# Products that share TensorE's array get priority behind the first of their group, and the projection's products come four steps later

## The chip, the cores and the metric

The kernel runs on one core of a Trainium2 chip. The metric is the device time of one execution in microseconds (us), lower is better. The profile is of one execution, taken by the hardware profiler; all times in it are counted from the first instruction.

## The reference

Three stages stand behind each other: soft-capped attention, an expert layer with a squared ReLU, and a soft mixture of eight experts.

```python
scores = scale * np.matmul(q, k.transpose(0, 1, 3, 2))     # q, k, v: (4, 12, 448, 64)
scores = cap * np.tanh(scores / cap)
attn = softmax(scores)                                      # denominator + 1e-9
attn_out = np.matmul(attn, v)
x = attn_out.transpose(0, 2, 1, 3).reshape(1792, 768)

h = x @ w_in                                                # w_in: (768, 2048)
g = s * np.maximum(h, 0.0) ** 2 + b
x2 = g @ w_out                                              # w_out: (2048, 768)

logits = x2 @ phi                                           # phi: (768, 32)
d = softmax(logits, axis=0); c = softmax(logits, axis=1)
slot_input = (d.T @ x2).reshape(8, 4, 768)
slot_out[e] = np.maximum(slot_input[e] @ w1[e], 0.0) @ w2[e]
return c @ slot_out.reshape(32, 768)
```

`w_in` and `w_out` arrive as 64-bit floats and are turned into 32-bit ones on the chip.

## The kernel before

A batch is 448 rows of `x`; there are four. The twelve heads of a batch are taken in three groups of four, so `Q` runs from 0 to 11 over groups, and the heads of a group are two pairs (`j` = 0, 1). A group is worked through in 16 steps (`s`).

*Scores.* The scores of a group stand transposed, keys on the partitions, in four chunks `c` of keys: three of 128 (`c` < `KF`), and a last one of 64 that the two heads of a pair share. q and k are split into a high and a low part (`qh`, `ql`, `kh`, `kl`), and a score is the sum of three products, kh·qh + kh·ql + kl·qh. The contraction is 64 long, so a product fills half of TensorE's rows, and the two heads of a pair (`i` = 0, 1) stand in the two halves of the rows. For the first six groups (`WIDE = 6`) `scores` computes one pair of one chunk at a time: six products. From group 6 on, `visit` computes both pairs of a chunk at once: twelve products, into two PSUM tiles with the tags `sc` and `U`; its last chunk is six products of full height. ScalarE takes tanh of them (line 141 or 168), then exp in place (line 206).

*U.* `weighted` multiplies the exponentials with v: for a chunk eight products, two halves `h` of a head's 64 columns times four heads `i`. A product's result is 32 columns wide, and the four heads go to the four quarters of TensorE's columns. It is called for one chunk at a time in the first batch, for chunks (0, 1) and (2, 3) in groups 3 to 5 (sixteen products each), and for all four chunks in groups 6 to 11 (thirty-two). `sums` adds the exponentials up (`Sm`, line 226), and `finish` divides and splits the result into the high and low part of `x`, which also frees the PSUM tile `U`.

*Hidden.* `hidden` computes `x @ w_in` of a batch in 16 chunks of 128 columns, 18 products each (line 527, `hp`), from weights that ScalarE and VectorE split just before (lines 511 and 512). `turn` transposes the squared ReLU (line 550, `tp`; ScalarE copies it away at line 552), and `post` makes the logits (line 564, `L`) four chunks at a time.

*Conversion.* During the first two batches a generator, `convert`, turns the weights into 32-bit floats on ScalarE (line 372) and VectorE (lines 377, 401, 405). w_out comes in eight units `fh` of 256 rows in one buffer `o`. When a unit is ready, `down` multiplies it with phi (line 457, `pp`, six products), `fold` folds that (`pf`), and three times `wturn` transposes a third of it (`tw`), ScalarE copies it back (line 477), and a DMA takes it to a scratch tensor in memory (line 478). The next unit's conversion waits for these DMAs, since there is one buffer `o`. The products are called through the list `self.later`; before it is worked off, the generator yields `HOLD` times. In the first two batches one `next(self.conv)` is made for each third of a chunk of hidden. After the last unit `bias` makes a sum of `pw` (`bp`).

*Order.* `block` weaves `hidden`, `post`, `attention` and `convert` together by calling their generators in turn. What is called earlier has the higher priority; a scheduler then lays out each engine's instructions in order, taking of those that its model holds ready the one of highest priority. On the chip each engine runs its list in that order. `high_priority(n)` moves what is made within it n places ahead, and `issue_after(x)` puts it behind x.

The last 110 us are the experts (`tail`), which stream 54 pieces of weights of 1 MB each (w_out, w1, w2); the first 17 are asked for during the fourth batch, one after another behind its products.

Of the kernel before, what the change touches and what calls it, by code (L numbers as in the profile page):

```python
# [17 lines left out]
P = 128  # L18
B, H, S, D = 4, 12, 448, 64
# [14 lines left out]
KF = S // P  # L34
# [6 lines left out]
LAST = 3  # L41
CASTS = 8
LEAD = 10
WIDE = 6
VISITS = (4, 7, 10, 13)
U = 256
CU = 768
HOLD = 2
XPOS = (1, 4, 7, 10, 13, 15, 15, 15)
POSTS = [[(), (), (0,), (1,)], [(-2,), (-1,), (0, 1), (2,)], [(-1,), (0,), (1,), (2,)], [(-1,), (0,), (1,), (2,)]]  # L50
OUT_GROUPS = [(0, 4), (4, 6)]
# [8 lines left out]
class Body:  # L60
    def __init__(self, nc, tc, io, consts, general, f64, wsc, osc):
        self.nc, self.tc, self.io, self.c, self.general = nc, tc, io, consts, general
        self.f64, self.wsc, self.osc = f64, wsc, osc
        self.ws, self.wr = {}, {}
        self.x = {}
        self.qk = {}
        self.r2 = {}
        self.e = {}
        self.v = {}
        self.nslot = 0  # L70
        self.later, self.wide, self.nsplit = [], False, 0
        self.nx = 0
        self.mark = None
        self.raws = 3

    def bank(self, name):
        return self.pst[0].tile([P, 512], F32, tag="T", bufs=self.pst[1], name=name)
# [48 lines left out]
    def scores(self, p, c):  # L126

        nc = self.nc
        Q, j = divmod(p, 2)
        qh, ql, kh, kl = self.qk[p]  # L130
        sc = (self.ps2 if self.ps2 is not None and j else self.psa).tile([P, 2, 512], F32, tag="sc", bufs=1, name="sc")
        for n, (k, q) in enumerate(((kh, qh), (kh, ql), (kl, qh))):
            if c == KF:
                nc.tensor.matmul(sc[:, 0, :S], k[:, KF * P:], q, start=(n == 0), stop=(n == 2))
            for i in range(2) if c < KF else ():
                r = slice(64 * i, 64 * i + 64)
                nc.tensor.matmul(sc[:, i, :S], k[r, c * P:(c + 1) * P], q[r, :], start=(n == 0), stop=(n == 2))  # L137
        if j == 0:
            self.e.setdefault(Q, []).append(self.ap.tile([P, 4 if c < KF else 2, S], F32, tag="e", bufs=4 if self.general else 3, name="e"))
        if c < KF:  # L140
            nc.scalar.activation(self.e[Q][c][:, 2 * j:2 * j + 2, :], sc[:, :, :S], AF.Tanh, scale=self.c["tsc"])  # L141
        else:
            nc.scalar.activation(self.e[Q][c][:, j, :], sc[:, 0, :S], AF.Tanh, scale=self.c["tsc"])
        if c == NCH - 1:
            del self.qk[p]

    def visit(self, Q, c):

        nc = self.nc
        t = [self.qk[2 * Q + j] for j in range(2)]  # L150
        if c == KF:
            sc = self.psa.tile([P, 2, 512], F32, tag="sc", bufs=1, name="sc")
            for j, (qh, ql, kh, kl) in enumerate(t):
                for n, (k, q) in enumerate(((kh, qh), (kh, ql), (kl, qh))):
                    nc.tensor.matmul(sc[:, j, :S], k[:, KF * P:], q, start=(n == 0), stop=(n == 2))
            self.e[Q].append(self.ap.tile([P, 2, S], F32, tag="er", bufs=1, name="er"))
            nc.scalar.activation(self.e[Q][c], sc[:, :, :S], AF.Tanh, scale=self.c["tsc"])
            del self.qk[2 * Q], self.qk[2 * Q + 1]
            return
        sc = [self.psa.tile([P, 2, 512], F32, tag=n, bufs=1, name="sc") for n in ("sc", "U")]  # L160
        for j, (qh, ql, kh, kl) in enumerate(t):
            for n, (k, q) in enumerate(((kh, qh), (kh, ql), (kl, qh))):
                for i in range(2):
                    r = slice(64 * i, 64 * i + 64)
                    nc.tensor.matmul(sc[j][:, i, :S], k[r, c * P:(c + 1) * P], q[r, :], start=(n == 0), stop=(n == 2))  # L165
        self.e.setdefault(Q, []).append(self.ap.tile([P, 4, S], F32, tag="e", bufs=3, name="e"))
        for j in range(2):
            nc.scalar.activation(self.e[Q][c][:, 2 * j:2 * j + 2, :], sc[j][:, :, :S], AF.Tanh, scale=self.c["tsc"])  # L168
# [65 lines left out]
    def weighted(self, Q, chunks):  # L234

        nc = self.nc
        if chunks[0] == 0:
            self.U = self.psa.tile([P, 2, 512], F32, tag="U", bufs=1, name="U")
        for k in chunks:
            for h in range(2):  # L240
                for i in range(4):
                    d = (i % 2 * KF + k if k < KF else 2 * KF) * D + 32 * h
                    nc.tensor.matmul(self.U[32 * i:32 * i + 32, h, :S], self.v[2 * Q + i // 2][self.rows(i, k), d:d + 32], self.chunk(4 * Q + i, k),  # L243
                                     start=(k == 0), stop=(k == KF))

    def finish(self, Q):

# [17 lines left out]
    def attention(self):  # L265
# [13 lines left out]
        for Q in range(last + 1):  # L279
            for s in range(2 * STEPS):  # L280
# [3 lines left out]
                elif Q < last:  # L284
# [5 lines left out]
                    self.between(Q, s)  # L290
                if not self.general and 0 < Q <= WIDE and s == 1:
                    self.add(Q - 1, 3)
                if not self.general and 0 < Q <= WIDE and s == 3:
                    self.sums(Q - 1)
# [4 lines left out]
    def wide_at(self, Q):  # L299

        return not self.general and Q >= WIDE

# [51 lines left out]
    def convert(self, units):  # L354
# [26 lines left out]
        for n in range(N + 1):  # L381
            if n:
                units[n - 1][2](out.pop(n - 1))
            late = n < N and n not in out
            for _ in range(HOLD if self.later and late else 0):
                yield
# [399 lines left out]
    def block(self, bi, atn):  # L786
# [5 lines left out]
        for grp in range(4):  # L792
# [6 lines left out]
            for k in range(12):  # L799
                next(h)  # L800
                next(post, None)
                if bi < 2:
                    next(self.conv, None)
                while done < min(total, (12 * grp + k + 1) * total / (48 - LEAD)):
                    next(atn)
# [242 lines left out]
```

## Time and profile before

| | |
|---|---|
| median of 3 runs | 642.76 us (639.36, 642.76, 643.01) |
| the profiled execution | 638.93 us, of which the span of its instructions is 637.2 |
| TensorE (PE) busy | 593.7 us, 93% of the span |
| ScalarE (ACT) busy | 402.1 us, 63% |
| VectorE (DVE) busy | 343.4 us, 54% |
| mean granted TensorE clock | 0.988 |

PE is TensorE's products, PEld its weight loads, which run beside the products. Products are pipelined, so a row's length is longer than what it costs: the cost of a piece of work is read from the start of its first row to the start of the next piece. The full-precision products (U, Sm, L, pp) leave two records each, those of scores and hidden one. In the rows' names buffer numbers are left out.

### The profile page before, as it was taken

To read this page: it belongs to the slowest core of one execution; us is meant where nothing else is said; L and a number is where in the kernel's file an instruction comes from. 1 tells how busy PE (TensorE), PEld (TensorE's weight loads), DVE (VectorE), ACT (ScalarE), POOL (GpSimd) and SP (SyncE) were. 2 spreads that over 40 slices of the span, in tenths; PEclk is the share of its full clock that TensorE was granted. 3 is DMA by queue.
4 is the path that set the end of the run, shared out by engine and by line. 5 is a ranking of instruction groups with operands and counts; after the bars stand their busy time and mean duration, and the time that the engine had idled before them with its cause. 6 is when DMAs were issued, how large, how long until landed. Compare 5 with 4: busy or idle time off the path is not lost.

```text
span 637.2 us, 11290 instructions
## 1 busy us (share of the span) xinstructions
PE 593.7 (93%) x4592; PEld 396.3 (62%) x4592; DVE 343.4 (54%) x509; ACT 402.1 (63%) x683; POOL 4.1 (1%) x11
## 2 busy tenths in 40 slices
PE   8898999999999999999999999999999998998672
PEld 5333575746776747567687476768868884346461
DVE  4998899878894482844624825454332224112121
ACT  5887889879867959679569386866645662001010
POOL 1000000000000000000000000000000000000000
PEclk9998999999999999999999999999999999999997
DMA  8843778786685442221421221211968859999998
GB/s 297 290 128 115 269 262 300 252 274 199 235 299 198 136 154 83 87 78 50 141 75 52 84 75 40 72 54 56 394 256 313 315 190 394 421 419 417 419 412 318
DMA packets 39626, 137.38 MB, mean 216 GB/s; under 512 B 4352, under 2 KB 12304, under 8 KB 32656
## 3 DMA queue, kind: packets, MB, share of 16 engines
q1 hardware_dynamic: 39280, 136.07, 59.2%
q8 instruction: 38, 0.62, 0.4%
q0 software_dynamic: 288, 0.53, 0.2%
q14 instruction: 20, 0.16, 0.1%
HBM read 118.49 MB, written 18.09 MB: 214 GB/s over the span
## 4 chain that ended last, share of the span: by engine, by line
PE 65%; DMA 14%; DVE 9%; ACT 8%; issue 3%; SPq 0%; DVEq 0%; ACTq 0%
PE hp L527 32%; DMA wt<-in_w_dram 12%; PE U L243 9%; PE tp L550 4%; PE sc L165 3%; PE pt L640 2%; PE L L564 2%; PE sc L137 2%; PE Sm L226 2%; ACT e L206 2%; ACT e L168 1%; PE tw L475 1%; DVE rec L232 1%; DMA osc<-o 1%; PE pp L457 1%
## 5 line engine op out<-in xcount | busy, mean ns | idle before, releaser
L527 PE MATMUL hp<-x,ws 128*128 128x448 f32 x1152 | 271.4, 376 | 0.0
L527 PEld LDWEIGHTS hp<-x,ws 128*128 128x128 f32 x1152 | 206.4, 188 | 42.2 <-issue 29.4
L512 DVE TENSOR_TENSOR ws<-wr,ws 128x384 fp32r<-128x384 f32 x128 | 70.6, 553 | 123.3 <-ACT ws L511 123.1
L511 ACT CAST ws<-wr 128x384 fp32r<-128x384 f32 x128 | 66.8, 524 | 36.8 <-PE hp L527 36.3
L243 PE MATMUL U<-e,v 128*32 128x448 f32 (+1 forms) x672 | 75.8, 551 | 4.7 <-ACT e L206 3.7
L206 ACT ACTIVATE e<-e,c_acap 128x1792 f32<-128x1792 f32 (+1 forms) x42 | 71.5, 1702 | 0.5
L552 ACT COPY g<-tp 112x256 f32<-112x256 f32 x128 | 43.3, 385 | 12.8 <-PE tp L550 12.0
L243 PEld LDWEIGHTS U<-e,v 128*32 128x32 f32 (+1 forms) x672 | 20.7, 110 | 45.4 <-issue 36.3
L232 DVE RECIPROCAL rec<-rec 128x448 f32<-128x448 f32 x12 | 35.4, 2950 | 18.1 <-ACT rec L231 18.1
L141 ACT ACTIVATE e<-sc,c_tsc 128x896 f32<-128x896 f32 x36 | 35.9, 1008 | 12.9 <-PE sc L137 11.9
L533 ACT ACTIVATE r<-hp 128x448 f32<-128x448 f32 x63 | 34.9, 554 | 9.8 <-PE hp L527 9.8
L550 PE MATMUL tp<-c_cst,r 128*112 128x128 f32 x256 | 39.0, 275 | 1.7 <-ACT g L552 1.4
L897 ACT COPY wt<-op 128x512 f32<-128x512 f32 x12 | 7.0, 586 | 50.6 <-PE op L892 50.6
L168 ACT ACTIVATE e<-sc,c_tsc 128x896 f32<-128x896 f32 x36 | 36.1, 1035 | 4.0 <-PE sc L165 4.0
L534 ACT ACTIVATE r<-r 128x448 f32<-128x448 f32 x63 | 37.6, 596 | 0.4
L912 PE MATMUL so_ps<-wt,free 128*32 128x128 f32 x768 | 26.5, 282 | 10.9 <-DMA wt<-in_w_dram 10.5
L550 PEld LDWEIGHTS tp<-c_cst,r 128*112 128x112 f32 x256 | 29.5, 133 | 11.3 <-ACT g L552 3.8
L215 DVE TENSOR_TENSOR es<-e 128x1792 f32<-128x1792 f32 x12 | 24.3, 2022 | 13.7 <-ACT e L206 13.7
L912 PEld LDWEIGHTS so_ps<-wt,free 128*32 128x32 f32 x768 | 20.8, 113 | 15.2 <-DMA wt<-in_w_dram 12.8
L215 DVE TENSOR_TENSOR es<-es,e 128x1792 f32<-128x1792 f32 x12 | 24.3, 2022 | 9.6 <-ACT e L206 9.6
L231 ACT ACTIVATE rec<-Sm,c_eps 128x448 f32<-128x448 f32 x12 | 7.7, 638 | 28.9 <-PE Sm L226 28.9
L863 PE MATMUL hps<-wt,free 128*32 128x512 f32 x192 | 21.0, 593 | 0.0
(186 smaller groups left out, 705.9 us busy)
## 6 DMA issues: line engine op xcount, KB each, us to landing
wt<-in_w_dram SPq DMA_DIRECT2D x48, 1024.0 KB, 16.5
wr<-wsc SPq DMA_DIRECT2D x48, 384.0 KB, 3.1
raw<-in_w_in_dram SPq DMA_DIRECT2D x16, 768.0 KB, 5.2
raw<-in_w_outT_dram SPq DMA_DIRECT2D x16, 768.0 KB, 5.8
wsc<-wr SPq DMA_DIRECT2D x16, 384.0 KB, 3.0
osc<-o SPq DMA_DIRECT2D x24, 256.0 KB, 2.9
wt<-osc SPq DMA_DIRECT2D x6, 1024.0 KB, 7.0
k<-in_kT_dram SPq DMA_DIRECT2D x22, 256.0 KB, 3.4
```

Source lines behind the costliest of these rows:

```text
L168: nc.scalar.activation(self.e[Q][c][:, 2 * j:2 * j + 2, :], sc[j][:, :, :S], AF.Tanh, scale=self.c["tsc"])
L206: ins = self.nc.scalar.activation(e, e, AF.Exp, scale=self.c["acap"]).ins
L215: self.nc.vector.tensor_add(es, e[0] if c == 1 else es, e[c])
L232: nc.vector.reciprocal(self.rec, self.rec)
L243: nc.tensor.matmul(self.U[32 * i:32 * i + 32, h, :S], self.v[2 * Q + i // 2][self.rows(i, k), d:d + 32], self.chunk(4 * Q + i, k), start=( ...
L511: self.nc.scalar.copy(hi, u)
L512: self.nc.vector.tensor_sub(lo, u, hi.bitcast(F32))
L527: nc.tensor.matmul(hp[:, :S], ws[kc // 3][:, w, kc % 3, :], x[:, s, kc, :], start=(k == 0), stop=(k == 3 * KC - 1))
L534: self.mark = nc.scalar.activation(r2, r2, AF.Square).ins
L550: self.nc.tensor.transpose(tp[:CP, q * P:(q + 1) * P], r2[:, q * CP:(q + 1) * CP], self.c["idn"])
L552: self.nc.scalar.copy(self.g[q][:CP, :, fc * P:(fc + 1) * P], tp[:CP, 2 * q * P:2 * (q + 1) * P].rearrange("p (a b) -> p a b", b=P))
L912: nc.tensor.matmul(so_ps[32 * e:32 * e + 32, G, :], ht[G][:, f, 32 * e:32 * e + 32], w2[f // 4][:, f % 4, e, :], start=(f == 0), stop=(f = ...
```

## The change

A helper `together` takes a list of products. It issues the first as before, and all others with a priority 3000 places ahead, and behind the first. The scores of pairs from the third on (`scores` with p ≥ 2, and `visit`) and U from group 3 on go through it. `visit` also takes the terms in another order, kl·qh first and kh·qh last, and in its last chunk the second pair first. `HOLD` becomes 4, so `down`, `fold` and `wturn` of a unit are called two steps of the generator later than before.

```diff
+VISIT = 3000
-HOLD = 2
+HOLD = 4
...
+    def together(self, products, near=True):
+
+        if not near:
+            products = [f() for f in products]
+            return
+        first, rest = products[0](), products[1:]
+        with self.tc.issue_after(first.ins), self.tc.high_priority(VISIT):
+            for p in rest:
+                p()
...
     def scores(self, p, c):
...
-        for n, (k, q) in enumerate(((kh, qh), (kh, ql), (kl, qh))):
-            if c == KF:
-                nc.tensor.matmul(sc[:, 0, :S], k[:, KF * P:], q, start=(n == 0), stop=(n == 2))
-            for i in range(2) if c < KF else ():
-                r = slice(64 * i, 64 * i + 64)
-                nc.tensor.matmul(sc[:, i, :S], k[r, c * P:(c + 1) * P], q[r, :], start=(n == 0), stop=(n == 2))
+        products = [lambda n=n, k=k, q=q, i=i, r=r: nc.tensor.matmul(sc[:, i, :S], k[r, c * P:(c + 1) * P], q[r, :], start=(n == 0), stop=(n == 2))
+                    for n, (k, q) in enumerate(terms) for i, r in halves]
+        if p < 2:
+            for f in products:
+                f()
+        else:
+            self.together(products)
...
     def visit(self, Q, c):
...
-            for j, (qh, ql, kh, kl) in enumerate(t):
-                for n, (k, q) in enumerate(((kh, qh), (kh, ql), (kl, qh))):
-                    nc.tensor.matmul(sc[:, j, :S], k[:, KF * P:], q, start=(n == 0), stop=(n == 2))
+            self.together([lambda j=j, n=n, k=k, q=q: nc.tensor.matmul(sc[:, j, :S], k[:, KF * P:], q, start=(n == 0), stop=(n == 2))
+                           for j, (qh, ql, kh, kl) in reversed(list(enumerate(t))) for n, (k, q) in enumerate(((kl, qh), (kh, ql), (kh, qh)))])
...
-        for j, (qh, ql, kh, kl) in enumerate(t):
-            for n, (k, q) in enumerate(((kh, qh), (kh, ql), (kl, qh))):
-                for i in range(2):
-                    r = slice(64 * i, 64 * i + 64)
-                    nc.tensor.matmul(sc[j][:, i, :S], k[r, c * P:(c + 1) * P], q[r, :], start=(n == 0), stop=(n == 2))
+        half = [slice(64 * i, 64 * i + 64) for i in range(2)]
+        self.together([lambda j=j, n=n, k=k, q=q, i=i, r=r: nc.tensor.matmul(sc[j][:, i, :S], k[r, c * P:(c + 1) * P], q[r, :], start=(n == 0), stop=(n == 2))
+                       for j, (qh, ql, kh, kl) in enumerate(t) for n, (k, q) in enumerate(((kl, qh), (kh, ql), (kh, qh))) for i, r in enumerate(half)])
...
     def weighted(self, Q, chunks):
...
+        self.together(products, Q >= 3)
```

Three places of TensorE's order show it; a row is a line of the program, the tile written and the tiles read, and how many such instructions follow each other.

TensorE at the second half of U of group 3, before; L is the first batch's logits, pp and tw belong to the unit of w_out that is being converted:

```order
L137 MATMUL sc<-qh,kh 128x448 x2
L243 MATMUL U<-e,v 32x448 x5
L137 MATMUL sc<-ql,kh 128x448 x2
L457 MATMUL pp<-o,c_misc 32x256 x6
L137 MATMUL sc<-qh,kl 128x448 x2
L243 MATMUL U<-e,v 32x448 x4
L475 MATMUL tw<-c_cst,o 128x128 x4
L243 MATMUL U<-e,v 32x448 x7
L527 MATMUL hp<-x_398,ws 128x448 x6
```

and now (the line numbers are those of the changed file):

```order
L237 MATMUL Sm<-es,c_ones 32x448
L256 MATMUL U<-e,v 32x448 x16
L237 MATMUL Sm<-es,c_ones 32x448 x3
L542 MATMUL hp<-x_398,ws 128x448 x6
L565 MATMUL tp<-c_cst,r_817 112x128 x4
L145 MATMUL sc<-qh,kh 128x448 x2
L145 MATMUL sc<-ql,kh 128x448 x2
L145 MATMUL sc<-qh,kl 128x448 x2
L472 MATMUL pp<-o,c_misc 32x256 x6
```

The sixteen products of U stand in one piece instead of three, and the six of the scores too.

TensorE in group 8, where a visit is cut by a transpose, before:

```order
L165 MATMUL sc<-qh,kh 128x448 x2
L165 MATMUL sc<-ql,kh 128x448 x2
L165 MATMUL sc<-qh,kl 128x448 x2
L165 MATMUL sc<-qh,kh 128x448 x2
L550 MATMUL tp<-c_cst,r_2269 112x128 x4
L165 MATMUL sc<-ql,kh 128x448 x2
L165 MATMUL sc<-qh,kl 128x448 x2
```

and now, in the same group:

```order
L175 MATMUL sc<-qh,kl 128x448 x2
L175 MATMUL sc<-ql,kh 128x448 x2
L175 MATMUL sc<-qh,kh 128x448 x2
L565 MATMUL tp<-c_cst,r_2162 112x128 x4
L542 MATMUL hp<-x_1095,ws 128x448 x10
L565 MATMUL tp<-c_cst,r_2246 112x128 x4
L542 MATMUL hp<-x_1095,ws 128x448
L175 MATMUL sc<-qh,kl 128x448 x2
L175 MATMUL sc<-ql,kh 128x448 x2
L175 MATMUL sc<-qh,kh 128x448 x2
```

The pieces are now of whole pairs of heads; the second pair of this visit stands behind ten products of hidden and a transpose.

TensorE between the last `tw` of the seventh unit of w_out and `pp` of the eighth, before:

```order
L475 MATMUL tw<-c_cst,o 128x128 x4
L155 MATMUL sc<-ql,kh 128x448
L155 MATMUL sc<-qh,kl 128x448
L527 MATMUL hp<-x_1095,ws 128x448 x2
L550 MATMUL tp<-c_cst,r_1747 112x128 x4
L527 MATMUL hp<-x_1095,ws 128x448 x4
L243 MATMUL U<-e,v 32x448 x24
L243 MATMUL U<-er,v 32x448 x8
L527 MATMUL hp<-x_1095,ws 128x448 x8
L457 MATMUL pp<-o,c_misc 32x256 x6
```

and now, where `tw`, ten products of hidden and six of scores stand just ahead of these rows:

```order
L542 MATMUL hp<-x_1095,ws 128x448 x19
L175 MATMUL sc<-qh,kl 128x448 x3
L175 MATMUL sc<-ql,kh 128x448 x2
L175 MATMUL sc<-qh,kh 128x448 x2
L175 MATMUL sc<-qh,kl 128x448
L175 MATMUL sc<-ql,kh 128x448 x2
L175 MATMUL sc<-qh,kh 128x448 x2
L542 MATMUL hp<-x_1095,ws 128x448
L175 MATMUL sc<-qh,kl 128x448 x2
L175 MATMUL sc<-ql,kh 128x448 x2
L175 MATMUL sc<-qh,kh 128x448 x2
L472 MATMUL pp<-o,c_misc 32x256 x6
```

U no longer stands between the two; scores and hidden do.

## Rows read from the trace of the kernel before

**Rows 1.** Busy time of each engine by stage: stretch, length, engines, granted clock, DMA

```profile
0.00:66.50 66.50, 57.80 (x419) 26.66 (x419) 54.00 (x78) 52.61 (x56) 2.98 (x9) 0.97 0.60 205
66.50:200.00 133.50, 131.94 (x850) 87.45 (x848) 112.89 (x142) 109.85 (x180) 0.00 (x0) 1.00 0.77 265
200.00:430.00 230.00, 226.46 (x1528) 152.22 (x1525) 121.84 (x166) 170.31 (x293) 0.54 (x1) 1.00 0.28 85
...
528.00:637.20 109.20, 79.66 (x1248) 50.05 (x1246) 23.89 (x64) 11.94 (x22) 0.54 (x1) 0.94 0.99 401
```

**Rows 2.** Who waited for whom, TensorE: us in total, times, longest

```profile
PE U L243 <- ACT e L206: 3.7, 3, 1.6
...
PE pp L457 <- DVE o L405: 2.8, 4, 1.4
...
PE tp L550 <- ACT g L552: 1.4, 3, 0.7
```

**Rows 3.** Groups by line, hidden: busy, mean ns, idle before

```profile
L527 PE MATMUL hp<-x,ws 128*128 128x448 f32 x1152 | 271.4, 376 | 0.0
```

**Rows 4.** Timeline of TensorE, start and length in us: U in one piece

```profile
116.52 3.21 PE L243 MATMUL U<-e,v 128*32 128x448 f32 x32
119.67 0.55 PE L475 MATMUL tw<-c_cst,o 128*128 128x128 f32 x3
```

**Rows 5.** Timeline of TensorE: U in three pieces

```profile
132.85 1.69 PE L243 MATMUL U<-e,v 128*32 128x448 f32 x10
134.47 0.47 PE L137 MATMUL sc<-ql,kh 64*128 64x448 f32 x2
...
136.26 1.82 PE L243 MATMUL U<-e,v 128*32 128x448 f32 x8
138.01 0.66 PE L475 MATMUL tw<-c_cst,o 128*128 128x128 f32 x4
138.60 1.70 PE L243 MATMUL U<-e,v 64*32 64x448 f32 x14
140.23 1.48 PE L527 MATMUL hp<-x,ws 128*128 128x448 f32 x6
```

**Rows 6.** Timeline of TensorE: a visit in two pieces, a transpose between

```profile
284.06 0.47 PE L165 MATMUL sc<-qh,kh 64*128 64x448 f32 x2
...
285.71 0.65 PE L550 MATMUL tp<-c_cst,r 128*112 128x128 f32 x4 [0.58 <-ACT g L552]
286.29 0.48 PE L165 MATMUL sc<-ql,kh 64*128 64x448 f32 x2
...
286.90 0.47 PE L527 MATMUL hp<-x,ws 128*128 128x448 f32 x1
```

**Rows 7.** Timeline of TensorE: a visit in one piece

```profile
292.74 0.47 PE L165 MATMUL sc<-qh,kh 64*128 64x448 f32 x2
...
294.15 0.47 PE L527 MATMUL hp<-x,ws 128*128 128x448 f32 x1
```

**Rows 8.** Timeline of TensorE: a transpose between products of hidden

```profile
295.48 0.60 PE L550 MATMUL tp<-c_cst,r 128*112 128x128 f32 x4
295.83 1.46 PE L527 MATMUL hp<-x,ws 128*128 128x448 f32 x6
```

**Rows 9.** Timeline of all engines: from the seventh unit's last tw to pp

```profile
219.24 0.60 PE L475 MATMUL tw<-c_cst,o 128*128 128x128 f32 x4
...
224.46 1.82 ACT L372 ACTIVATE o<-raw 128x768 f32<-128x768 f32 x2 [0.27 <-DMA osc<-o]
...
230.50 1.06 PE L457 MATMUL pp<-o,c_misc 128*32 128x256 f32 x12 [0.42 <-DVE o L405]
```

**Rows 10.** Waits of SP's DMA queue

```profile
SPq L725 <- DVE ws L512: 11.8, 1, 11.8
```

**Rows 11.** Chain that ended last, its pieces in the tail: start, length in us

```profile
547.52 13.68 DMA wt<-in_w_dram
```

**Rows 12.** Timeline of TensorE: U of group 2, behind a wait

```profile
51.33 3.77 PE L243 MATMUL U<-e,v 128*32 128x448 f32 x16 [0.93 <-DVE c_hh L255]
```

More of the change, by code (lines that the diff above doesn't have):

```diff
@@ L131, in scores @@
         sc = (self.ps2 if self.ps2 is not None and j else self.psa).tile([P, 2, 512], F32, tag="sc", bufs=1, name="sc")
-        for n, (k, q) in enumerate(((kh, qh), (kh, ql), (kl, qh))):
-            if c == KF:
-                nc.tensor.matmul(sc[:, 0, :S], k[:, KF * P:], q, start=(n == 0), stop=(n == 2))
-            for i in range(2) if c < KF else ():
-                r = slice(64 * i, 64 * i + 64)
-                nc.tensor.matmul(sc[:, i, :S], k[r, c * P:(c + 1) * P], q[r, :], start=(n == 0), stop=(n == 2))
+        halves = [(0, slice(0, P))] if c == KF else [(i, slice(64 * i, 64 * i + 64)) for i in range(2)]
+        terms = ((kh, qh), (kh, ql), (kl, qh))
+        products = [lambda n=n, k=k, q=q, i=i, r=r: nc.tensor.matmul(sc[:, i, :S], k[r, c * P:(c + 1) * P], q[r, :], start=(n == 0), stop=(n == 2))
[5 more added lines that the diff above has]
+            self.together(products)
         if j == 0:
@@ L238, in weighted @@
             self.U = self.psa.tile([P, 2, 512], F32, tag="U", bufs=1, name="U")
-        for k in chunks:
+        order = tuple(chunks)
+        products = []
+        for k in order:
             for h in range(2):
@@ L242, in weighted @@
                     d = (i % 2 * KF + k if k < KF else 2 * KF) * D + 32 * h
-                    nc.tensor.matmul(self.U[32 * i:32 * i + 32, h, :S], self.v[2 * Q + i // 2][self.rows(i, k), d:d + 32], self.chunk(4 * Q + i, k),
-                                     start=(k == 0), stop=(k == KF))
+                    products.append(lambda k=k, h=h, i=i, d=d: nc.tensor.matmul(
+                        self.U[32 * i:32 * i + 32, h, :S], self.v[2 * Q + i // 2][self.rows(i, k), d:d + 32], self.chunk(4 * Q + i, k),
+                        start=(k == 0), stop=(k == KF)))
+        self.together(products, Q >= 3)
     def finish(self, Q):
```

## Prediction

> **What bounds the kernel now.** I read the stages first [rows 1]. In the stretch from 66.5 to 200 us TensorE is busy for 131.9 of 133.5 us, from 200 to 430 us for 226.5 of 230: together it idles 5.1 us in 363.5. VectorE is busy for 85% of the first of these stretches and ScalarE for 82%, in the second for 53% and 74%. So TensorE's own list is the time there, and the other two have some room, least before 200 us. The groups by line confirm it: hidden's products never wait, 0.0 us before 1152 of them [rows 3]. The waits that TensorE does have are few: 2.8 us at pp for VectorE's last step on a unit of w_out, 1.4 us at transposes for ScalarE's copy, and 3.7 us at U for exp, these before 25 us [rows 2].
>
> Busy is not the same as used. Sixteen products of U in one piece take 116.52 to 119.67, 3.15 us or 0.79 for four [rows 4]: the four heads run side by side in the quarters of the columns. Where a piece is cut in the middle of a four, the rest of the four is alone and the row still counts as busy. The same holds for scores, whose two heads run side by side. That is what this change can win, and it is read from starts of pieces, not from busy time.
>
> In the last stage the weights of the experts set the time: the DMA engines are 99% busy at 401 GB/s, and the chain there goes through these loads [rows 1, 11]. They begin when buffers of the fourth batch come free: SP's queue of them stands 11.8 us for VectorE's last splits of hidden's weights [rows 10]. So the stage starts when hidden ends, and I let all that is won before it arrive at the end.
>
> **U in one piece.** Before, the second half of U of group 3 stands in three pieces: 132.85 to 134.47, 136.26 to 138.01 and 138.60 to 140.23, together 5.00 us [rows 5], against 3.15 whole [rows 4]: 1.85 us lost. Three more of the twelve U from group 3 on are cut, at 153.70, 175.22 and 351.13; read in the same way they lose 0.85, 0.29 and 0.86. The order now has all twelve whole. Sum: **−3.85 us**, all on TensorE's path.
>
> **Scores in one piece.** A whole visit takes 292.74 to 294.15, 1.41 us for six pairs of products [rows 7]; a piece of two pairs takes 286.29 to 286.90, 0.61 [rows 6]. Solved for both, a pair costs 0.20 and every new piece 0.21. Counted in the two orders from the first product of hidden on, scores stand in 65 pieces before and in 50 now: 15 × 0.21 = 3.1. Six pairs of heads are cut apart before and one now; a cut pair runs as two products of 0.20: 5 × 0.20 = 1.0. Sum **−4.1 us**. The order of the terms, low part first, adds no instruction. It makes the first product wait for the part that is ready last, so that those behind it need no wait of their own; no row before shows a visit of group 6 or later waiting for an operand, so I give it nothing, between 0 and −0.5.
>
> **What moves next to them.** A transpose ahead of hidden costs 0.35 us (295.48 to 295.83 [rows 8]), ahead of scores 0.58 (285.71 to 286.29 [rows 6]). Such neighbours fall from 15 to 8: −1.6 at most; I take −1.2, since some of these 15 cost less than the one shown. Hidden itself stands in 154 pieces instead of 151, 3 × 0.2 = +0.6 at the price of a piece of scores, an estimate. Sum **−0.6 us**.
>
> **Phi's products later.** Two more steps of the generator are two thirds of a chunk of hidden, so `pp` of the second and third unit now has scores or some eight products of hidden more ahead of it. Both waited for VectorE. Of the four waits, 2.8 us in total and the longest 1.4 [rows 2], I expect three to go: −2.4. The fourth, the last unit's, gets worse. From the seventh unit's last tw to that pp it takes 11.26 us [rows 9]: tw, ScalarE's copy, the DMA, whose end releases ScalarE at 224.46, and then 6.04 us of ScalarE and VectorE until pp starts. The tw of the seventh unit is itself later now, and what lies between is 30 products of hidden and 24 of scores in three pieces: 0.35 + 30 × 0.20 + 12 × 0.20 + 3 × 0.21 = 9.4 us. So pp would wait for 11.3 − 9.4 = 1.9 us, instead of 0.4. Sum −2.4 + 1.5 = **−0.9 us**; with the chain at its shortest and all other waits gone −2.8, with a busier VectorE there (U's division and split now stand among its steps) +1. On SP's queue a unit's three stores come later with their tw and change places with loads of q, k, v and of weights by a few rows; hidden, whose weights go through that queue, does not wait now [rows 3], and I give it nothing. `pf`, `bp` and the logits behind it come later too, by up to two chunks of hidden. ScalarE writes a chunk's squared ReLU into one of nine buffers, which the transposes behind the logits free; in the new order the relu of the chunk ten places on stands right behind that transpose. It holds no product of hidden back as long as the other of two PSUM tiles is free, and thirty-two products of U (two of rows 4's pieces, 6.3 us) stand there as cover. I take 0; without that cover it is one wait for ScalarE, 0.7 us if it is as long as the longest at a transpose [rows 2].
>
> **Waits at transposes.** The transpose in [rows 6] waited 0.58 us for ScalarE behind a cut visit, one of three such waits, 1.4 us in total [rows 2]. Transposes still follow visits at several places, so I take half: **−0.7 us**, between 0 and −1.4.
>
> **The first 66 us.** Here VectorE (54.0) and ScalarE (52.6 of 66.5 us) count as much as TensorE. Two single pieces of scores between U's of group 1 and 2 go, 0.4 us each, half of it on the path: **−0.4 us**. The granted clock has a mean of 0.97 here [rows 1], and U of group 2, directly behind a wait of 0.93 us, takes 3.77 us for eight products, where rows 4 have 1.6: it runs at the lower level, 1.2 GHz [rows 12]. Two products of scores now stand ahead of that U and shorten the wait; whether the clock then stays at 2.4 GHz no row says. I take 0, between 0 and −2.2 (3.77 − 1.6).
>
> **New waits.** TensorE's list is shorter by ten us and ScalarE's and VectorE's are not. One place is plain in the order: a visit's second half in group 8 needs the PSUM tile U back, whose sums `Sm` now come some 15 us behind U. The nearest rows are the 5.1 us that TensorE idles in both stretches [rows 1]. I take **+1.5 us**, between 0 and another 5.
>
> **Sum.** −3.85 − 4.1 − 0.6 − 0.9 − 0.7 − 0.4 + 1.5 = −9.05, say −9.1 us. The profiled execution took 638.93 (637.2 of span and 1.7 around it), which gives 629.8. It is at the low end of the runs shown; taken from their median, 642.76, the forecast is **633.7 us**. With the bounds above (−15 to −4) its own range is 628 to 639.
>
> **Rivals.**
>
> *The win turns into waits.* Of the sum, about 5.5 us lie before 200 us (3.0 of U, 1.5 of scores, 1.0 of pp). There VectorE is 85% and ScalarE 82% busy and each of them has its own long operations; if TensorE, 4% earlier, only waits for them, that part is lost and −3.5 us stay: 639. For it: pp's waits are for VectorE. Against it: hidden never waits [rows 3], and shortening 133.5 us by 5.5 puts VectorE at 88%, not at 100. The Trainium skill (TensorEngine Tiling (Array Packing), Performance Considerations, PSUM Bottleneck) says that packing small products speeds up TensorE but not the evacuation of PSUM, which may then become the limit; that speaks for this rival. By that rule the trace of before shows only the start, the 1.4 us at transposes for ScalarE's copy.
>
> *The end does not follow.* If the last stage's loads were paced by memory from the fourth batch on, 99% busy as the DMA engines are, TensorE's gain would end in a longer wait for weights: −1 to 0, 642. Against it: the wait of 11.8 us of their queue for hidden [rows 10].
>
> *Slower: U waits for exp.* Priority draws the products of U for the last chunk right up to the exponentials. TensorE takes its list in order, so each of the twelve U from group 3 on can stand for ScalarE with hidden's products behind it. If ScalarE is late by more than the 4.7 us that the first 24 products of a U take (three quarters of two of rows 4's pieces), each such U waits, as long as the longest wait of U for exp before, 1.6 us in the first stage [rows 2]: 12 × 1.6 = 19 less the 10.6 won, **+9**, 652. Against it: ScalarE at 74% from 200 us on, and before too U starts close behind the last scores.
>
> **Chances.** The forecast 0.62, more than it 0.05, the win turned into waits 0.20, an end that does not follow 0.06, slower through U 0.07. About 1% (6.4 us) is what a measurement of this kernel can tell from no change. Faster by over 1%: the forecast and the case above it, less 0.05 for the part of the forecast's own range that wins under 6.4 us, 0.62; within 1%: that part, the waits and the end that does not follow, 0.31; slower: 0.07. For the range, forecast and waits together hold 0.82: 625 to 642.
>
> **What would show it.** In the changed kernel's trace U from group 3 on should stand in pieces of 3.15 and 6.3 us and visits in 1.4; hidden should still wait 0.0; pp's waits should be one, of 1 to 3 us, near 230 us; the first load behind hidden should start some 9 us earlier. I would be wrong if TensorE's idle time from 66.5 to 430 us grew by more than 5 us, or if the stage of the experts grew longer than 109 us.

## The result and the profile after

| | before | after |
|---|---|---|
| median, this comparison (6 runs each) | 641.84 us (639.36 to 643.01) | 634.48 us (632.77 to 637.68) |
| profiled execution, its span | 638.93, 637.2 | 632.77, 630.9 |
| ratio, 95% interval | | 0.9896 (0.9864 to 0.9928) |
| first product of hidden starts at | 66.49 | 64.26 |
| `ln_ps`, the first products behind the last logits, start at | 528.53 | 522.10 |
| between the two | 462.0 | 457.8 |

The kernel is faster by 1.0%. The same kernel in a second comparison gave 635.14 against 640.62 (below, 0.9931), so the gain is 5.5 to 7.4 us. One execution of hold2, an experiment below, took 1965.88 us; it stands in that kernel's median and not in its ratio.

The first view is the busy time by stage, to be laid beside [rows 1]; the columns are the same.

```profile
0.00:66.50 66.50, 58.71 (x432) 27.98 (x434) 56.37 (x79) 53.91 (x58) 2.99 (x9) 0.95 0.64 217
66.50:200.00 133.50, 131.64 (x870) 89.19 (x867) 111.30 (x143) 114.19 (x185) 0.00 (x0) 1.00 0.76 263
200.00:430.00 230.00, 225.80 (x1532) 151.54 (x1531) 126.38 (x169) 168.42 (x294) 0.54 (x1) 1.00 0.28 84
```

From 66.5 to 430 us TensorE idles 1.9 + 4.2 = 6.1 us, where it was 5.1. ScalarE, the fourth busy time of a row, does more in the second stage than before (114.2 against 109.9), since more of the work now lies there; VectorE a little less. The waits of TensorE, as in [rows 2] (us in total, times, longest):

```profile
PE tp L565 <- ACT g L567: 2.9, 4, 0.9
...
PE U L256 <- ACT e L217: 1.3, 2, 0.9
PE sc L175 <- ACT e L179: 1.1, 2, 0.9
...
PE pp L472 <- ACT g L567: 0.4, 1, 0.4
...
PE pp L472 <- DVE o L420: 0.3, 1, 0.3
```

The product with phi has lost its 2.8 us of waiting for VectorE, and transposes have gained: 2.9 instead of 1.4, all for ScalarE's copy. Visits, of which no wait is listed before, wait 1.1 us for a tanh. U waits for exp at 12.8 and 22.2 us alone. The pieces themselves are as forecast, all but one U (at 129.87 us, shown with sums_too). TensorE's timeline, start and length, shows a U of two chunks from 168.91 to 172.19, 3.28 us, and a U of four from 414.36 to 420.64, 6.28 us ([rows 4]: 3.15 for two), and a whole visit from 406.25 to 407.68, 1.43 ([rows 7]: 1.41):

```profile
168.91 3.35 PE L256 MATMUL U<-e,v 128*32 128x448 f32 x32
172.19 0.66 PE L490 MATMUL tw<-c_cst,o 128*128 128x128 f32 x4
```

```profile
406.25 0.47 PE L175 MATMUL sc<-qh,kl 64*128 64x448 f32 x2
...
407.68 1.49 PE L542 MATMUL hp<-x,ws 128*128 128x448 f32 x6
...
414.36 4.72 PE L256 MATMUL U<-e,v 128*32 128x448 f32 x48
419.01 1.71 PE L256 MATMUL U<-er,v 64*32 64x448 f32 x16
420.64 0.96 PE L237 MATMUL Sm<-es,c_ones 128*32 128x448 f32 x8
```

For the sum by kind I take, for each product of TensorE, the time from its start to the next start, from the first product of hidden to `ln_ps`. Waits are then with the product ahead of them.

| us | before | after | difference |
|---|---|---|---|
| U | 60.65 | 57.63 | −3.0 |
| scores | 57.04 | 52.35 | −4.7 |
| transposes of hidden | 26.25 | 25.30 | −0.95 |
| hidden | 256.63 | 260.67 | +4.0 |
| all else | 61.5 | 61.9 | +0.4 |
| sum | 462.0 | 457.8 | −4.2 |

So U and scores give 7.7 us, and hidden takes back 4.0. Hidden's products take 0.202 us each when nothing holds them; what they take beyond that, by what comes behind the piece, goes from 0.5 to 4.0 us ahead of transposes, from 2.9 to 5.2 ahead of scores, and from 3.9 to 0.7 ahead of the product with phi.

Some of this only changes its place. Before, the transposes that waited stood behind scores, and their waits count there; now they stand behind hidden. So I also take the waits out: for each, the time from the start ahead of it to the start behind it, less what the same two kinds take where nothing waits. Then scores go from 54.5 to 50.85 us (−3.65), hidden from 253.0 to 253.85 (+0.85), and the waits from 6.5 to 8.7 (+2.2); those at transposes from 2.3 to 3.85. The idle time of the profile goes from 5.2 to 6.2 in the same stretch and shows less of it: a row of hidden is 0.376 us long [rows 3] while the next product can start after 0.202, so some 0.17 us of a wait behind it lie under the row.

Three of the new places, in the timelines of all engines. At 333 us:

```profile
331.32 1.94 ACT L179 ACTIVATE e<-sc,c_tsc 128x896 f32<-128x896 f32 x2
...
333.10 0.69 ACT L567 COPY g<-tp 112x256 f32<-112x256 f32 x2
...
333.85 0.65 PE L565 MATMUL tp<-c_cst,r 128*112 128x128 f32 x4 [0.86 <-ACT g L567]
```

The visit comes whole now, and here its two tanh stand directly ahead of the copies that free the tile for the next transpose: 1.94 us of ScalarE. Between the first product of hidden and `ln_ps` that is so at four places, and at none before. But it holds for two of the four waits alone (201.4 and 333.9, 1.57 of the 2.9 us). At 290.2 the copies stand behind three short steps for hidden (288.20 to 289.50), and at 153.2 behind a step of the conversion that itself waited for a store:

```profile
151.72 0.90 ACT L387 ACTIVATE o<-raw 128x768 f32<-128x768 f32 x1 [1.65 <-DMA osc<-o]
152.52 0.62 ACT L567 COPY g<-tp 112x256 f32<-112x256 f32 x2
...
153.19 0.54 PE L565 MATMUL tp<-c_cst,r 128*112 128x128 f32 x3 [0.65 <-ACT g L567]
```

Before, at the longest of these waits, the copies stood behind an exp, nearly as long as two tanh, and a split of weights:

```profile
339.38 1.79 ACT L206 ACTIVATE e<-e,c_acap 128x1792 f32<-128x1792 f32 x1
...
341.48 0.64 ACT L552 COPY g<-tp 112x256 f32<-112x256 f32 x2
...
342.17 0.54 PE L550 MATMUL tp<-c_cst,r 128*112 128x128 f32 x3 [0.71 <-ACT g L552]
```

The third place is at 234 us, where the last unit of w_out is converted:

```profile
229.99 1.69 ACT L387 ACTIVATE o<-raw 128x768 f32<-128x768 f32 x2 [1.62 <-DMA osc<-o]
231.59 0.89 ACT L91 CAST x<-U 128x896 fp32r<-128x896 f32 x1
232.38 0.51 ACT L526 CAST ws<-wr 128x384 fp32r<-128x384 f32 x1
232.79 1.00 ACT L179 ACTIVATE e<-sc,c_tsc 128x896 f32<-128x896 f32 x1
...
233.85 0.67 PE L175 MATMUL sc<-qh,kl 64*128 64x448 f32 x3 [0.87 <-ACT e L179]
```

ScalarE is busy without a gap, and the tanh that frees the scores' PSUM tile is the fourth in its row. The end follows in full. The first load of the chain in the tail (start, length) begins 6.4 us earlier than in [rows 11], and from there to the span's end it is 89.8 us, 89.7 before:

```profile
541.10 13.68 DMA wt<-in_w_dram
```

### The profile page after: what moved, and what is told of

Read it like the earlier page. It is cut to its first block, busy times and chain, and to the rows that moved or that the text cites. A ratio compares the mean times of both kernels' runs of the same rounds, so it can differ in the third digit from the quotient of the medians.

```text
span 630.9 us, 11279 instructions
## 1 busy us (share of the span) xinstructions
PE 587.1 (93%) x4592; PEld 393.5 (62%) x4592; DVE 343.5 (54%) x509; ACT 401.5 (64%) x683; POOL 4.1 (1%) x11
## 4 chain that ended last, share of the span: by engine, by line
PE 58%; DMA 15%; ACT 15%; DVE 8%; issue 3%; SPq 0%; ACTq 0%; DVEq 0%
PE hp L542 29%; DMA wt<-in_w_dram 12%; PE U L256 8%; PE tp L565 4%; ACT e L217 4%; PE sc L175 2%; PE pt L655 2%; ACT e L155 2%; PE L L579 2%; DMA osc<-o 2%; PE Sm L237 2%; ACT e L179 1%; ACT ws L526 1%; PE sc L145 1%; PE tw L490 1%
## 5 line engine op out<-in xcount | busy, mean ns | idle before, releaser
L527 DVE TENSOR_TENSOR ws<-wr,ws 128x384 fp32r<-128x384 f32 x128 | 70.3, 552 | 109.9 <-ACT ws L526 107.3
L526 ACT CAST ws<-wr 128x384 fp32r<-128x384 f32 x128 | 66.6, 524 | 32.7 <-PE hp L542 32.2
L256 PE MATMUL U<-e,v 128*32 128x448 f32 (+1 forms) x672 | 71.0, 551 | 2.1 <-ACT e L217 1.3
L145 PE MATMUL sc<-qh,kh 64*128 64x448 f32 (+1 forms) x84 | 22.2, 464 | 3.6 <-ACT e L155 1.7
L145 PEld LDWEIGHTS sc<-qh,kh 64*128 64x128 f32 (+1 forms) x84 | 9.4, 192 | 19.5 <-issue 6.3
```

The source lines that it names most:

```text
L145: products = [lambda n=n, k=k, q=q, i=i, r=r: nc.tensor.matmul(sc[:, i, :S], k[r, c * P:(c + 1) * P], q[r, :], start=(n == 0), stop=(n == ...
L256: products.append(lambda k=k, h=h, i=i, d=d: nc.tensor.matmul(self.U[32 * i:32 * i + 32, h, :S], self.v[2 * Q + i // 2][self.rows(i, k), d ...
L526: self.nc.scalar.copy(hi, u)
L527: self.nc.vector.tensor_sub(lo, u, hi.bitcast(F32))
```

## The experiments

Those of one group were timed on one chip beside the kernel before, g_both_first on another; the first row has the medians of before beside the change, the three groups and g_both_first. "Stretch" is the time from the first product of hidden to `ln_ps` in the profiled execution, "first" where it begins, "tp" the waits at transposes for the copy `g`, "pp" those at the product with phi.

| kernel | median us | ratio (95%) | first | stretch | tp | pp |
|---|---|---|---|---|---|---|
| before | 641.84, 640.53, 640.62, 640.94, 640.45 | | 66.5 | 462.0 | 1.4 | 2.8 |
| the change | 634.48 | 0.9896 (0.9864 to 0.9928) | 64.3 | 457.8 | 2.9 | 0.7 |
| hold2 | 634.44 | 0.9893 (0.9861 to 0.9926) | 63.8 | 457.9 | 1.9 | 3.8 |
| hold4_only | 642.37 | 1.0027 (1.0008 to 1.0046) | 65.5 | 465.4 | 2.2 | 1.3 |
| u_only | 640.65 | 0.9998 (0.9976 to 1.0019) | 66.6 | 460.3 | 1.7 | 3.6 |
| scores_only | 635.76 | 0.9924 (0.9894 to 0.9953) | 63.9 | 459.5 | 2.2 | 2.8 |
| changed_again | 635.14 | 0.9931 (0.9908 to 0.9954) | 65.0 | 458.0 | 2.8 | 0.9 |
| early_as_before | 634.86 | 0.9924 (0.9903 to 0.9945) | 65.2 | 458.4 | 2.8 | 0.7 |
| high_first | 633.46 | 0.9895 (0.9879 to 0.9912) | 63.8 | 458.6 | 2.7 | 0.3 |
| g_on_dve | 633.87 | 0.9919 (0.9887 to 0.9950) | 63.9 | 458.7 | 3.3 | 0.5 |
| g_both_dve | 632.11 | 0.9873 (0.9847 to 0.9899) | 65.9 | 456.1 | 1.2 | 2.2 |
| g_first | 633.00 | 0.9879 (0.9852 to 0.9907) | 63.9 | 457.1 | 2.7 | 1.4 |
| sums_too | 634.95 | 0.9913 (0.9882 to 0.9943) | 65.9 | 458.5 | 3.3 | 0.9 |
| g_both_first | 631.20 | 0.9857 (0.9836 to 0.9879) | 64.0 | 457.4 | 1.5 | 2.1 |

The first group takes the change apart: grouping of U, grouping of scores, and the four steps.

**hold2**, the change with the old `HOLD`.

```diff
-HOLD = 4
+HOLD = 2
```

> The changed kernel with HOLD back at 2: products stay together, phi's products come as early as before. My account: the gain is mostly the pieces of scores and U and the clock in the first stage; only pp's waits come back, 2 to 3 us, so the ratio to the kernel before is about 0.994 (-4 us) and the wait at pp for VectorE is 2 to 3 us again. Rival, the gain is HOLD's: ratio 0.998 to 1.0.

It is as fast as the change, where the account had 4 us for it and the ratio 0.994. The product with phi waits again, and the transposes wait less by 1 us; the stretch is the same to 0.1 us. The change's waits at 153.2 and 201.4 us, 1.36 us together, are not there; one of 0.71 at 242.6 is new.

```profile
PE pp L472 <- DVE o L420: 2.8, 4, 1.5
PE tp L565 <- ACT g L567: 1.9, 3, 0.9
...
PE pp L472 <- ACT r L549: 1.0, 1, 1.0
```

**hold4_only**, the kernel before with `HOLD = 4` and nothing else.

```diff
-HOLD = 2
+HOLD = 4
```

> The kernel before with HOLD 4 alone. Its order has U from group 3 on in 23 pieces instead of 17 and scores in 62 instead of 65. My account: pp's waits go (-3 us), the six new pieces of U cost 2 to 4 us, so the ratio is 0.997 to 1.002. Rival, the gain is HOLD's: ratio 0.992 or less.

Slower by 0.3%, just outside the account's range, and by 3.3 us in the stretch, though the product with phi waits 1.5 us less: U is cut into more pieces, and its sum by kind is 2.9 us longer, that of `tw` 1.2; that of scores is the same.

**u_only**, U grouped from group 3 on, scores and `HOLD` as before; the edit is shown against the change, and `visit` is put back likewise.

```diff
-        self.together(products)
+        for n, (k, q) in enumerate(((kh, qh), (kh, ql), (kl, qh))):
...
-HOLD = 4
+HOLD = 2
```

> The kernel before with U from group 3 on together, nothing else. My account: -3 to -4 us for the five pieces fewer, ratio 0.995; pp's waits and the clock in the first stage as before. Rival, U's products then wait for exp: U's waits over 2 us more than before and a ratio of 1.0 or more.

U takes 3.7 us less, as forecast for it (3.85), and scores 1.3 more, 1.0 of which are waits behind them; the product with phi waits 0.8 more. The stretch is shorter by 1.7. Of that the medians show nothing (between −1.5 and +1.2 us). The account's ratio is missed; the rival's 1.0 came, but without its cause, since U waits for exp less than before (2.9 us instead of 3.7).

**scores_only**, scores grouped, U and `HOLD` as before.

```diff
-        self.together(products, Q >= 3)
+        self.together(products, False)
...
-HOLD = 4
+HOLD = 2
```

> The kernel before with scores together (and low part first), U and HOLD as before. My account: 16 pieces fewer, -4 us, the clock in the first stage -2 us, waits at transposes +1.5, so ratio 0.993. Rival, what grouped scores win they give back in waits for ScalarE: ratio 0.998 to 1.0, with 3 us or more of waits at transposes and scores.

Scores take 5.6 us less, hidden 3.9 more; with the waits taken out scores take 3.9 less and hidden the same, and the waits grow by 2.9. The stretch falls by 2.5, and the first product of hidden comes 2.6 earlier. This part alone gives most of the change's time. In the stretch the parts add up where `HOLD` is left alone: −1.7 − 2.5 = −4.2, and hold2, which has both, −4.1.

The second group asks what the first stage and the order of the terms are worth, and tries to take ScalarE out of the waits at transposes.

**changed_again**, the change once more, as a measure for the others. 

> The changed kernel once more, as the yardstick of this chip: ratio 0.99, -6 to -7 us; waits at transposes near 3 us and none over 0.5 us at pp, if these are of the program and not of one execution.

Medians of one kernel differ by 0.7 us between the two comparisons, and those of the kernel before by up to 1.4; less than that is not told from noise below.

**early_as_before**, the scores of pairs up to the sixth left as they were.

```diff
-        if p < 2:
+        if p < 6:
```

> The changed kernel with the scores of the first three groups issued as before: TensorE's order up to the first product of hidden is that of the kernel before, behind it that of the changed one. My account: the clock falls again at U of group 2, hidden starts 2 us later, ratio 0.9925. Rival, the clock's fall is chance or hidden in a stage bound by ScalarE and VectorE: ratio 0.9895 to 0.9905, first product of hidden at 64 to 65 us.

The time is that of the change once more, and so is the stretch. The ratio is the one that the account gave, but the fall of the clock that it gave as the reason did not come. Of interest is the clock from 48 to 58 us, where the kernel before ran U of group 2 at the lower level [rows 12]. The windows of 48 to 58 us, of before and of this kernel (the third number from the end is the granted clock):

```profile
48.00:58.00 10.00, 8.56 (x53) 3.10 (x50) 7.05 (x6) 6.76 (x6) 0.00 (x0) 0.83 0.37 126
```

```profile
48.00:58.00 10.00, 8.58 (x66) 3.35 (x66) 8.39 (x9) 8.13 (x9) 0.00 (x0) 1.00 0.36 126
```

With the early scores ungrouped the clock stays up here; it does so in hold4_only too. So what rows 12 show does not come with that order of TensorE every time.

**high_first**, the terms of `visit` in the old order.

```diff
-for n, (k, q) in enumerate(((kl, qh), (kh, ql), (kh, qh)))
+for n, (k, q) in enumerate(((kh, qh), (kh, ql), (kl, qh)))
```

> The changed kernel with visit's terms in the old order, kh first. My account: the order of the terms is worth nothing, ratio within 0.001 of the changed kernel's. Rival, the low part first spares waits within a visit: 1 to 2 us slower, with waits of scores for VectorE's kl in groups 6 to 11.

No loss; its median is below changed_again's by 1.7 us, its stretch the longer one by 0.6. The account's 0.001 is missed beside changed_again (0.9931) and met beside the first comparison (0.9896). The low part first wins nothing that shows; whether the old order is a little faster is not settled, since the two intervals touch.

**g_on_dve**, the second of the two copies behind a transpose on VectorE, from the ninth chunk on and not in the last batch.

```diff
-            self.nc.scalar.copy(self.g[q][:CP, ...
+            (self.nc.vector.tensor_copy if q and 16 * bi + fc >= 8 and bi < B - 1 else self.nc.scalar.copy)(self.g[q][:CP, ...
```

> The changed kernel with one of a transpose's two copies out of PSUM on VectorE instead of ScalarE, from the ninth chunk of hidden to the end of the third batch. My account: the waits at transposes are for ScalarE, which has a visit's tanh and exp ahead of the copies, so they fall from 2.9 to under 1.5 us and the ratio to 0.986 to 0.988. Rival, they come from the order itself (one PSUM bank, transposes six products apart): waits and time stay, 0.989 to 0.991.

The waits did not fall, and the reason is in the timeline of the same place, 333 us:

```profile
330.77 1.93 ACT L179 ACTIVATE e<-sc,c_tsc 128x896 f32<-128x896 f32 x2
...
332.55 0.41 ACT L567 COPY g<-tp 112x256 f32<-112x256 f32 x1
...
333.00 0.42 DVE L567 COPY g<-tp 112x256 f32<-112x256 f32 x1 [1.98 <-ACT g L567]
333.48 0.65 PE L565 MATMUL tp<-c_cst,r 128*112 128x128 f32 x4 [0.80 <-DVE g L567]
```

VectorE's copy waits 1.98 us for ScalarE's: both read the same PSUM tile, and in the built kernel the second waits for the first. ScalarE's tanh are still in the way, so this run did not test what it was made for.

The third group does it properly, and tries two other repairs.

**g_both_dve**, both copies on VectorE.

```diff
-            self.nc.scalar.copy(self.g[q][:CP, ...
+            (self.nc.vector.tensor_copy if 16 * bi + fc >= 8 and bi < B - 1 else self.nc.scalar.copy)(self.g[q][:CP, ...
```

> Both copies behind a transpose are made by VectorE instead of ScalarE from the ninth chunk of hidden on, in the first three batches; all else as in the change. My account: the waits at transposes (2.9 us in the changed kernel, 1.4 before) come from ScalarE, whose two tanh of a whole visit stand ahead of the copies, so that the tile of the transpose comes free late; with VectorE copying they should fall to 1 us or less, and the time by 1 to 2 us against the change, to 633 to 634 beside a kernel before of 641, ratio 0.988. Rival, the waits change their engine: VectorE is busy for 111 of 133.5 us before 200 us and has its own long steps (converted weights, U's division and split), so that the transposes wait for VectorE as much as they did for ScalarE: waits at transposes of 2.5 us or more, time as the change, ratio 0.990 to 0.993, or slower where the splits of weights come late, up to 0.995.

The waits at transposes are 1.2 us, the stretch is 1.7 us shorter than the change's, and the median 2.4 to 3.0 us lower; with each gain taken against the kernel before on the same chip, 1.5 to 3.4 (the interval overlaps that of the change, not that of changed_again). With the waits taken out as above, they make 1.2 of the 1.7 us, 7.5 instead of 8.7; the rest may come from TensorE's order, which is another here. At the same place the tanh still take 1.90 us, and no transpose waits:

```profile
331.18 0.75 DVE L567 COPY g<-tp 112x256 f32<-112x256 f32 x2
...
332.01 1.90 ACT L179 ACTIVATE e<-sc,c_tsc 128x896 f32<-128x896 f32 x2
...
333.76 0.60 PE L565 MATMUL tp<-c_cst,r 128*112 128x128 f32 x4
```

The account holds in this: the waits at transposes were for ScalarE's queue. That two tanh made all of them does not hold, as 153.2 and 290.2 us of the change show. Half of the rival came true with it, at another place: the product with phi waits 1.3 us for a copy that VectorE makes only after four steps of w_out's conversion, from 207.19 us on, of which the last two are shown.

```profile
208.93 1.82 DVE L420 SCALAR_TENSOR_TENSOR o<-raw,o 128x768 int32<-128x768 int32 x2
...
211.14 0.74 DVE L567 COPY g<-tp 112x256 f32<-112x256 f32 x2
...
212.03 0.84 PE L472 MATMUL pp<-o,c_misc 128*32 128x256 f32 x10 [1.31 <-DVE g L567]
```

**g_first**, both copies on ScalarE, 3000 places ahead.

```diff
+        with self.tc.high_priority(VISIT) if bi < B - 1 else nullcontext():
             for q in range(2):
                 self.nc.scalar.copy(self.g[q][:CP, ...
```

> ScalarE's two copies behind a transpose get the same priority (3000 places ahead) as the products of a visit, so that they stand ahead of the exponentials and of a tanh that is not yet ready. My account: waits at transposes fall from 2.9 us, but only those in which an exp or a tanh of a later visit stood ahead; two tanh whose scores were done earlier still do: 1 to 2 us stay, and TensorE's order changes with it. Time 0.5 to 1.5 us below the change, ratio 0.987 to 0.990. Rival, ScalarE's time is only passed on: its list is as long as before, so that what the copies win exp and tanh lose, and U or scores wait by the same amount: waits at transposes below 2 us, but waits at scores and U above the 4.1 us of the change by as much; ratio 0.990 to 0.993.

The waits at transposes stay at 2.7 us, and those at scores fall (by starts, from 2.3 to 1.0), so neither account has the mechanism right. At 330.32 and 198.95 us of this run the two tanh stand ahead of the copies as before. The time, 1.5 to 2.1 us under the change's medians, cannot be laid to those waits; the stretch is 0.7 shorter, and the interval takes in the change.

**sums_too**, the four `Sm` grouped too. In the change the first of them stands alone ahead of a U at 129.87, and this U takes 3.98 us to the start of the other three, 0.83 more than in [rows 4]:

```profile
129.86 0.54 PE L237 MATMUL Sm<-es,c_ones 128*32 128x448 f32 x1
129.87 0.58 PE L256 MATMUL U<-e,v 128*32 128x448 f32 x3
...
130.27 3.65 PE L256 MATMUL U<-e,v 128*32 128x448 f32 x29
133.85 0.95 PE L237 MATMUL Sm<-es,c_ones 128*32 128x448 f32 x6
134.73 1.07 PE L542 MATMUL hp<-x,ws 128*128 128x448 f32 x4
```

```diff
-        for i in range(4):
-            nc.tensor.matmul(Sm[32 * i:32 * i + 32, :S], ...
+        self.together([lambda i=i: nc.tensor.matmul(Sm[32 * i:32 * i + 32, :S], ...
+                       for i in range(4)], Q >= 3)
```

> The four sums of the exponentials go through the helper too, from group 3 on, so that U no longer stands between the first sum and the other three (as at 130 us in the changed kernel, where that cost 0.84 us over the price of the pieces). My account: that place and the like win 0.5 to 1 us, waits elsewhere as they are: ratio 0.988 to 0.990, U's and the sums' starts together 0.8 us shorter. Rival: the sums are on full height and one piece more or less of them costs nothing: ratio and sums within 0.2 us of the change, 0.990 to 0.993.

No gain. The order only changed the cut: at that place one product of U now stands between the first sum and the other three, and the four sums and U take 5.44 us (132.01 to 137.45), in the change 4.87 (129.86 to 134.73):

```profile
132.01 0.92 PE L236 MATMUL Sm<-es,c_ones 128*32 128x448 f32 x2
132.76 0.92 PE L256 MATMUL U<-e,v 128*32 128x448 f32 x2
...
137.45 0.88 PE L542 MATMUL hp<-x,ws 128*128 128x448 f32 x3
```

**g_both_first**, both copies on VectorE and 3000 places ahead.

```diff
+        with self.tc.high_priority(VISIT) if bi < B - 1 else nullcontext():
             for q in range(2):
                 (self.nc.vector.tensor_copy if 16 * bi + fc >= 8 and bi < B - 1 else self.nc.scalar.copy)(...
```

> VectorE makes both copies behind a transpose, as in the run with both copies on VectorE (ratio 0.987, waits at transposes 0.8 us, one of 1.3 us at a product with phi for a copy that stands behind four steps of w_out's conversion), and they get the priority of a visit, which in VectorE's order puts that copy two conversion steps ahead. My account, waits on a copy can be placed away: the 1.3 us at the product with phi falls below 0.5, transposes stay at 1 us or less, time 0.5 to 1.5 us below that run, 631 to 632 beside a kernel before of 641, ratio 0.984 to 0.987. Rival, the unit of w_out that steps aside is then the later one: that product waits for the conversion instead, by the 0.7 us of the two copies or more; ratio as that run, 0.987 to 0.990.

The lowest median of all, 631.20, and below all other kernels here, though its interval still overlaps the change's. At 211 us the copy has stepped ahead, and the product with phi waits for the conversion instead, 0.83 in place of 1.31:

```profile
208.77 0.75 DVE L568 COPY g<-tp 112x256 f32<-112x256 f32 x2
...
209.44 1.81 DVE L420 SCALAR_TENSOR_TENSOR o<-raw,o 128x768 int32<-128x768 int32 x2
...
211.40 1.06 PE L472 MATMUL pp<-o,c_misc 128*32 128x256 f32 x12 [0.83 <-DVE o L420]
```

That is the rival's mechanism, at a smaller price. The stretch of this profile is 1.3 us longer than that of g_both_dve, its first stage 1.9 shorter; whether the priority adds anything to the move to VectorE is not settled.

## Why the prediction was right, and where it was not

The forecast was 633.7 us, and the kernel took 634.48 and 635.14. The gain, forecast at 9.1, was 5.5 to 7.4. Part of the nearness is luck: the three runs of before which the forecast was taken from had a high median, 642.76, where the later ones had 640.45 to 641.84. Taken from the profiled execution it was 629.8, and that of the change took 632.77. Two errors also cancel in part: the stretch gave 4.2 us of the 8.65 forecast for it, the first 66 us gave 2.2 instead of 0.4.

*The pieces* were right. U with −3.85 came out at −3.0, of which the cut at 129.87 explains the missing 0.8, and at −3.7 in u_only. Scores with −4.1 came out at −4.7, but 1.05 of that are waits that stand elsewhere now; without waits it is −3.65, and −3.9 in scores_only. Prices solved from starts of pieces, where busy time would have shown nothing, carried to the changed order. What moves next to them, −0.6, came to −0.1: transposes −0.95, but hidden without its waits +0.85, since scores or U follow it at 45 places instead of 39. The order of the terms, between 0 and −0.5, won nothing that shows.

*The waits* were the step that failed. With −0.7 at transposes, −0.9 at the product with phi and +1.5 for new ones the sum had −0.1; they came to +2.2, and that is half of the 4.5 us by which the stretch fell short. Those at transposes did not halve, they grew by 1.5 (1.4 to 2.9 in the profile). The reason given, that grouped visits stand apart from transposes, looked at TensorE's list alone. A transpose waits for the copies that free its tile, and these queue on ScalarE: at two places behind the two tanh of a whole visit, at two behind other steps. That ScalarE's queue holds them is shown: g_both_dve, with the copies on VectorE, has 1.2 us of these waits instead of 2.9 and is 2.4 to 3.0 us faster. That the grouping made this queue worse is argued from two tanh directly ahead of the copies at four places instead of none; no run moves the copies in the kernel before, so how much VectorE would win there is open. The Trainium skill's rule (TensorEngine Tiling (Array Packing), Performance Considerations, PSUM Bottleneck), that evacuation of PSUM may become the limit and both ScalarE and VectorE should be used for it, agrees with these numbers where VectorE takes both copies of a tile; with one on each engine the waits were 3.3 us. As a rival it stood with 0.20 and 639 us, the whole win before 200 us lost; it came as a part of the win, on both sides of 200 us (transposes wait at 153.2 and 201.4, and at 290.2 and 333.9). The new wait that I had placed, of a visit for the sums of U in group 8, is in no row; visits wait for a tanh at 234 and 236 us instead, 0.87 and 0.18.

*Phi four steps later*, −0.9, did take its waits away, more than I said: 2.8 to 0.7 us, and the last unit's 1.9 did not come, since TensorE stood 0.87 us for a tanh just ahead. But it was worth nothing: hold2 is as fast, with the waits back at that product and fewer at transposes and scores, and by itself `HOLD = 4` costs 3.3 us of the stretch. I had priced the step on the order of the whole change, where U can no longer be cut, and not what else fills the place.

*The first 66 us*, −0.4, gave −2.2 in the profile. Grouped early scores without a fall of the clock begin hidden at 63.8 to 64.0 (six kernels), ungrouped ones at 65.2 and 65.5 (early_as_before, hold4_only): −1.4 is the grouping's. The rest is the fall of before at 51 us [rows 12], about 1.1, less what the change lost in an own fall near 11 us, about 0.4. The medians don't show the −1.4 (changed_again and early_as_before 0.3 apart), so its part in the total is not settled.

*The rivals.* The end does follow: −6.4 us at `ln_ps`, −6.2 in the time. U waits for exp at no place from group 3 on. The win did turn into waits in part, 2.3 of the forecast's 8.65 in the stretch. Of what was to show it, U's and the visits' lengths, hidden's 0.0 and an idle time grown by less than 5 us came as said; the wait near 230 us came at scores and not at phi's product, and the first load 6.4 us earlier, not 9.

What stays open: where the waits of ScalarE's copies would stand without whole visits, and whether the first 66 us count in the medians.

## What to carry to other kernels

Price a cut in products that share the array from starts: here such prices of 4 us held to half a microsecond with the waits counted apart, and to 0.9 where another cut came in. But a change that makes one engine's work come in blocks can make its consumers' work come in blocks too; for each block, ask which engine takes it off and what small step that frees a buffer for the first engine is queued behind it there. Move that step to the engine with room, all of it, since half of it waits for the other half.

## What the hardware showed besides

TensorE's granted clock fell to its lower level, 1.2 GHz, at other places in other executions. Before had it at 51 us for 3.4 us, the change at 10.8 us for 6.8, the change once more at 19.2 us for 3.4, and eight of the other kernels at no place before 68 us. In windows from 8 to 24 us (granted clock third from the end), the change in its two profiles:

```profile
8.00:24.00 16.00, 13.51 (x86) 6.25 (x88) 12.36 (x20) 14.39 (x16) 0.00 (x0) 0.79 0.91 339
```

```profile
8.00:24.00 16.00, 11.24 (x80) 5.68 (x84) 11.43 (x19) 13.71 (x15) 0.00 (x0) 0.89 0.88 331
```

A fall costs 0.4 to 2 us at the first product of hidden, so a term read from one profile's first stage is uncertain by that much.
